# Bringing the second head group's routing chain forward in a list-scheduled attention kernel

## The chip, the cores and the metric

The kernel runs on one core of one Trainium2 chip. The metric is the time on the device in microseconds (us), and lower is better.

## The reference

Attention with 4 batches, 8 heads, 768 rows and 64 columns per head. Each query and key is assigned to the nearest of 16 centroids of its head, and a query sees only keys of its own cluster. The result goes through a gate with a long convolution (projection, convolution over the sequence, product, output projection).

```python
q_assign = np.argmax(np.einsum('bhsd,hcd->bhsc', q_n, c_n), axis=-1)      # q_n, k_n, c_n: normalised
k_assign = np.argmax(np.einsum('bhsd,hcd->bhsc', k_n, c_n), axis=-1)
mask = q_assign[:, :, :, None] == k_assign[:, :, None, :]
scores = np.where(mask, scale * np.matmul(q, k.transpose(0, 1, 3, 2)), -1e9)
attn = softmax(scores)                                                     # cut
x = (attn @ v) in rows of 512
proj = x @ w_proj; x1, x2, x3 = thirds of proj
y = x1 * irfft(rfft(x2) * rfft(filter)) * x3
out = y @ w_out
```

## The kernel before

The eight groups (n = 0 to 7) are four heads each, in two pairs. The kernel does not write its order down. It lists some 1,900 operations, each with an engine (or several to choose from), a guessed duration, a due time and its dependences. A list scheduler simulates the engines and takes, on the engine that is free first, the ready operation with the lowest due time. The order that comes out is what the engines run. The due times are corrected by a table of constants that was found by search, `NUDGE`.

```python
# Plan.op
o.due += NUDGE.get(o.seq, 0.0)
# Plan.place: of the operations that can start now, take the one that is due first
c = min((c for c in cand if c[0] <= t0 + wait + 1e-9), key=lambda c: (
    c[1].due - (bonus if e == "PE" and st.kind == "pv" == c[1].kind else 0.0)
    + (shape if e == "PE" and array(c[1], st.last) != st.last else 0.0)
    + (BUSY if e == "DVE" and len(c[1].eng) > 1 else 0.0) + (c[0] - t0) * 20, c[1].seq))
# Plan.done: when the scheduler believes that a DMA has landed
o.end = st.bw[e] + 0.6 + o.lat
```

The routing chain of a group, for n > 0: similarities of q and k to the centroids on TensorE, transposed on TensorE, the one-hot of the largest on VectorE, a DMA that transposes the one-hot, and eight small DMAs that write its rows ("mask rows") under q and k in the buffers `aug`. A score product over 80 rows (64 of q and k, 16 of the mask) then does the masking. A group's first scores wait for all of this.

```python
# routing(n), cut
b0 = end - 24.00965
op(("PE", 1.33), sim, b0, ...)                    # similarities
op(("PE", .68), simT, b0 + 2.5, ...)              # transposed
...                                               # one-hot on VectorE, due b0 + 3.3 to b0 + 4.2
due = b0 + 7.5
op(("SP", .6), lambda e: T.nc.sync.dma_start_transpose(T.ohT..., T.oh...), due - 2, ..., lat=1.0)
masks(n, range(2), due + 1.3)                     # eight DMAs from ohT to aug, lat=1.0
# the casts that put q and k in aug: whichever of the two engines the scheduler takes
op({"ACT": .83, "DVE": .5}, lambda e, ...: copy(e, T.augs[a][hp][j]..., T.qkT[z]...), due + 8 if n else due + 6, ...)
```

Loads of q, k and v for later groups and the small DMAs of the softmax denominators are issued by SyncE too, in one queue with the transpose and the mask rows.

The softmax here doesn't subtract the row's maximum and nothing guards it: scores larger than these inputs give would overflow.

## Time and profile before

| | before |
|---|---|
| median of 3 runs | 389.62 us (388.48 to 390.36) |
| span of the profiled run | 387.5 us |

The prediction below says how TensorE's idle time is spread over the kernel. It comes from the busy time in windows, two of which follow: the idle time is the stretch less TensorE's busy time, here 40 - 37.80 = 2.20 and 45 - 43.31 = 1.69 us. A line gives the stretch, its length, the busy us of TensorE, of its weight loads, of VectorE, ScalarE and GpSimd (with the number of instructions), the granted clock, the busy share of the DMA engines and their GB/s:

```profile
25.00:65.00 40.00, 37.80 (x299) 18.89 (x297) 34.54 (x42) 31.57 (x62) 2.68 (x5) 1.00 0.73 152
65.00:110.00 45.00, 43.31 (x334) 21.27 (x332) 40.19 (x47) 35.93 (x70) 0.00 (x0) 1.00 0.51 121
```

For comparing orders I use a second measure, the time from the second group's similarity products to the third group's, on TensorE's timeline (start, busy, instruction):

```profile
32.66 1.50 PE L584 MATMUL bank<-qkT,cbd 128*32 128x384 f32 x16
...
73.96 1.50 PE L584 MATMUL bank<-qkT,cbd 128*32 128x384 f32 x16
```

This stage takes 73.96 - 32.66 = 41.30 us, and both of the stops that the prediction starts from lie in it. It is called the second group's stage below.

### The profile page before, as it was taken

To read this page: it belongs to the slowest core of one execution; us is meant where nothing else is said; L and a number is where in the kernel's file an instruction comes from. 1 tells how busy PE (TensorE), PEld (TensorE's weight loads), DVE (VectorE), ACT (ScalarE), POOL (GpSimd) and SP (SyncE) were. 2 spreads that over 40 slices of the span, in tenths; PEclk is the share of its full clock that TensorE was granted. 3 is DMA by queue.
4 is the path that set the end of the run, shared out by engine and by line. 5 is a ranking of instruction groups with operands and counts; after the bars stand their busy time and mean duration, and the time that the engine had idled before them with its cause. 6 is when DMAs were issued, how large, how long until landed. Compare 5 with 4: busy or idle time off the path is not lost.

```text
span 387.5 us, 8477 instructions
## 1 busy us (share of the span) xinstructions
PE 367.5 (95%) x3251; PEld 212.4 (55%) x3256; DVE 353.9 (91%) x509; ACT 269.5 (70%) x514; POOL 46.8 (12%) x92
## 2 busy tenths in 40 slices
PE   2999996999999999999999999999999999999995
PEld 1565452455445555555454555555455566568893
DVE  8898996899799999999998999999999999999782
ACT  5897786788894887788874976778865567632342
POOL 8501000000002010101010100101010100000400
PEclk9999999999999999999999999999999999999999
DMA  9829972750668659866797596845646551110214
GB/s 176 180 65 210 215 170 53 176 142 23 167 125 162 127 83 184 105 147 78 166 162 185 76 246 119 139 90 69 131 64 186 59 162 12 44 43 2 94 72 162
DMA packets 93860, 47.17 MB, mean 122 GB/s; under 512 B 82088, under 2 KB 87676, under 8 KB 93820
## 3 DMA queue, kind: packets, MB, share of 16 engines
q1 hardware_dynamic: 87836, 36.84, 42.1%
q0 software_dynamic: 2704, 8.98, 16.5%
q10 hardware_dynamic: 3280, 0.82, 1.2%
q8 instruction: 25, 0.41, 0.5%
q14 instruction: 15, 0.12, 0.1%
HBM read 31.59 MB, written 7.40 MB: 101 GB/s over the span
## 4 chain that ended last, share of the span: by engine, by line
PE 54%; DVE 24%; DMA 9%; issue 5%; SPq 5%; ACT 3%; DVEq 0%; POOL 0%; POOLq 0%
PE bank L73 19%; PE pair L681 17%; DVE acc L695 8%; PE bank L807 5%; PE bank L71 4%; DMA rb<-dr 3%; PE bank L555 2%; DMA aug<-ohT 2%; PE bank L584 2%; DMA ohT<-oh 2%; SPq L461 2%; DVE tm L831 1%; SPq L746 1%; DVE x L871 1%; SPq L294 1%
## 5 line engine op out<-in xcount | busy, mean ns | idle before, releaser
L681 PE MATMUL pair<-p,vraw 128*64 128x385 f32 x768 | 142.7, 490 | 0.3
L670 ACT ACTIVATE p<-bank 128x512 f32<-128x512 f32 x192 | 113.8, 612 | 36.9 <-PE bank L73 34.4
L695 DVE TENSOR_TENSOR acc<-p,acc 128x1536 f32<-128x1536 f32 x64 | 112.0, 1749 | 3.4 <-ACT p L670 1.1
L681 PEld LDWEIGHTS pair<-p,vraw 128*64 128x64 f32 x768 | 53.0, 136 | 51.0 <-issue 45.8
L73 PE MATMUL bank<-aug,aug 80*64 80x512 bf16 (+3 forms) x590 | 69.0, 327 | 5.2 <-DMA aug<-ohT 3.1
L667 ACT ACTIVATE p<-bank 128x512 f32<-128x512 f32 x96 | 58.8, 612 | 1.7 <-PE bank L73 1.0
L73 PEld LDWEIGHTS <-aug 80*64 80x64 bf16 (+1 forms) x590 | 34.2, 109 | 37.3 <-issue 21.6
L729 POOL DMA_DIRECT2D acc<-acc x30 | 23.8, 795 | 244.1 <-DVE acc L695 81.9
L73 PE MATMUL bank<-xT,wpj 128*64 128x384 bf16 x424 | 41.3, 326 | 0.0
L260 ACT COPY qkT<-bank 128x384 f32<-128x384 f32 x62 | 27.9, 496 | 13.2 <-PE bank L73 8.9
L73 PEld LDWEIGHTS <-wpj 128*64 128x64 bf16 x424 | 27.4, 109 | 13.0 <-issue 7.0
L695 DVE TENSOR_TENSOR acc<-p,p 128x1536 f32<-128x1536 f32 x16 | 28.0, 1750 | 2.1 <-ACT p L670 2.0
L73 PEld LDWEIGHTS <-y 128*64 128x64 bf16 x448 | 24.7, 110 | 8.7 <-issue 3.0
L831 DVE TENSOR_TENSOR tm<-bank,hm 128x512 f32<-128x512 f32 x44 | 27.6, 678 | 0.8 <-ACT p L670 0.4
L260 ACT CAST aug<-qkT 64x768 bf16<-64x768 f32 x29 | 24.0, 830 | 3.0 <-PE bank L73 2.6
L807 PE MATMUL bank<-wpj,xT 128*64 128x512 bf16 x192 | 21.6, 379 | 0.8 <-DVE xT L775 0.8
L73 PE MATMUL bank<-wout,y 128*64 128x512 bf16 x176 | 21.2, 379 | 0.0
L71 PE MATMUL bank<-aug,aug 128*128 128x256 bf16 (+3 forms) x87 | 19.3, 320 | 0.6 <-DVE x L871 0.2
L260 ACT COPY tm<-bank 128x512 f32<-128x512 f32 x14 | 8.0, 589 | 16.1 <-PE bank L807 9.7
L555 PE MATMUL bank<-ident,qkraw 128*128 128x128 f32 x144 | 19.2, 278 | 0.0
L555 PEld LDWEIGHTS bank<-ident,qkraw 128*128 128x128 f32 x144 | 15.6, 140 | 6.3 <-issue 4.2
L262 DVE CAST aug<-qkT 64x768 bf16<-64x768 f32 x31 | 17.6, 572 | 1.5 <-PE bank L73 0.9
(149 smaller groups left out, 434.9 us busy)
## 6 DMA issues: line engine op xcount, KB each, us to landing
vraw<-in_v_dram SPq DMA_DIRECT2D x16, 384.0 KB, 3.5
qkraw<-in_q_dram SPq DMA_DIRECT2D x30, 192.0 KB, 4.8
qkraw<-in_k_dram SPq DMA_DIRECT2D x30, 192.0 KB, 5.2
rb<-dr SPq DMA_DIRECT2D x30, 192.0 KB, 3.6
out_dram<-ob SPq DMA_DIRECT2D x11, 512.0 KB, 3.7
acc<-acc POOLq DMA_DIRECT2D x10, 384.0 KB, 4.9
acc<-acc POOLq DMA_DIRECT2D x10, 192.0 KB, 4.1
y<-in_moe_filter_fft_dram SPq DMA_DIRECT2D x4, 384.0 KB, 7.3
```

Source lines behind the costliest of these rows:

```text
L71: return T.nc.tensor.matmul(out, lhsT, rhs, start=start, stop=stop)
L73: T.nc.tensor.matmul(out[64 * i:64 * i + 64], lhsT[:, 64 * i:64 * i + 64], rhs, start=start, stop=stop)
L260: T.nc.scalar.copy(out, in_)
L262: (T.nc.vector if e == "DVE" else T.nc.gpsimd).tensor_copy(out, in_)
L555: T.nc.tensor.transpose(bank(h.ids[i // 3])[:, ts(i % 3, 128)], raw(s, i), T.ident)
L667: T.nc.scalar.activation(o, ap(h).rearrange("p (a b) -> p a b", a=2), Act.Exp, scale=0.125)
L670: T.nc.scalar.activation(flat(s)[:, lo:lo + 512], ap(h), Act.Exp, scale=0.125)
L681: T.nc.tensor.matmul(o[64 * hp:64 * hp + 64, ch, :385], T.vraw[vs][:, hp, sk * D:(sk + 1) * D], T.p[slots[sk]][:, hp, 384 * ch:384 * ch + ...
L695: T.nc.vector.tensor_tensor(T.acc[os], P_(t[0]), P_(t[1]) if len(t) == 2 else T.acc[os], op=Alu.add)
L729: op(("POOL", .8), lambda e, rows=rows: T.nc.gpsimd.dma_start(flat_()[:rows], flat_()[rows:2 * rows], accum_op=Alu.add), te, r=[], w=[("ac ...
L807: T.nc.tensor.matmul(ap(h)[64 * i:64 * i + 64], T.xT[xs][:, kt, c:c + 64], T.wpj[:, kt, DM:2 * DM], start=kt == 0, stop=kt == ND - 1)
L831: op(("DVE", .68), lambda e, i=i, cs=cs, r=r, h=h: T.nc.vector.tensor_tensor(T.tm[r][:, cs], ap(h), hmrow(i, (0, 2, 2, 3)[2 * r + cs]), op ...
```

## The change

Going by the edit, the intent is to make the second group's one-hot earlier, since its masks come late, and to tell the scheduler that the first transposes and mask rows take longer to land than it believes, so that it issues them sooner. Because every change of the plan moves everything behind it, the due times were then searched for anew.

```diff
-LEAD = 1.97516
+LEAD = 2.99901
-BUSY = 8.32578
+BUSY = 8.09741
+EARLY = 8.73655
-NUDGE = {10:3.7,75:-1.5,90:7.4, ...          (142 entries, cut)
+NUDGE = {6:-0.2,9:0.7,10:3.7,11:-0.3, ...    (271 entries, cut: 136 unchanged, 6 changed, 129 new)
...
-    ... bonus=11.03330, margin=0.02203, shape=1.60501):
+    ... bonus=10.84378, margin=0.02195, shape=1.63806):
...
     # mask rows
-    ... byts=25e3, lat=1.0))
+    ... byts=25e3, lat=2.0 if n < 3 else 1.0))
...
-        b0 = end - 24.00965
+        b0 = end - 24.04235
+        b0 -= EARLY * (n == 1)
...
     # transpose of the one-hot
-    ... byts=196e3, lat=1.0)
+    ... byts=196e3, lat=3.0 if n < 3 else 1.0)
...              (T0, TAU1, w0, w1 moved by under 1 us; w0 of the last batch from -8.47659 to -4.47412)
```

No arithmetic is added or removed. What changes is the order on each engine, and in some cases the engine.

More of the change, by code (lines that the diff above doesn't have):

```diff
@@ L35 @@
 ROWS = 16
-LEAD = 1.97516
+LEAD = 2.99901
 FIRST = 2
-BUSY = 8.32578
+BUSY = 8.09741
 HELD = 4
-NUDGE = {10:3.7,75:-1.5,90:7.4,91:7.4,129:-0.8,140:0.4,156:6.6,187:-5.6,193:0.1,212:-0.2,216:15.5,218:8.0,222:-3.8,243:1.1,253:-4.1,255:-7.1,256:-7.1,257:-3.0,264:4.3,274:2.3,281:0.9,288:9.1,289:11.6,328:-9.2,363:0.5,370:2.2,378:0.5,379:0.7,400:-0.2,406:1.5,409:-4.8,434:0.6,440:-3.7,479:0.8,480:-0.3,481:-1.3,494:-0.6,495:-4.2,508:-1.9,511:-0.2,518:-5.0,524:0.5,526:2.1,539:-2.3,554:10.5,568:1.6,573:0.4,587:-4.9,590:0.2,597:-2.4,617:0.7,620:-1.0,658:0.8,664:0.1,684:2.2,690:-8.8,740:1.0,759:0.5,767:0.4,779:-0.7,782:1.7,788:0.7,790:0.8,826:-0.5,828:-0.3,848:-2.2,872:-1.3,883:-5.3,888:-3.6,897:-0.8,898:-1.1,901:-3.5,915:-3.1,941:0.4,947:-0.4,969:-0.8,996:2.0,997:2.0,1026:2.7,1029:-2.1,1039:2.0,1043:-1.2,1048:1.2,1056:10.8,1062:0.4,1066:0.9,1098:-1.0,1101:0.3,1118:-2.2,1127:1.5,1130:-1.5,1143:-2.6,1194:-0.9,1255:0.7,1257:0.7,1263:0.3,1270:-0.2,1271:-1.1,1276:-3.6,1295:4.9,1317:-2.0,1321:0.4,1351:5.6,1373:-1.5,1441:9.4,1450:3.5,1461:2.0,1478:-1.3,1501:-8.3,1546:0.2,1557:0.1,1563:-0.6,1624:2.8,1630:-1.5,1634:0.3,1640:-4.0,1641:-4.0,1642:-13.7,1643:-4.0,1655:-4.1,1666:0.5,1685:-2.9,1771:-3.3,1776:0.2,1788:-7.8,1797:0.1,1808:-0.1,1809:-0.1,1827:-0.7,1841:-1.3,1844:0.9,1862:-0.4,1863:2.1,1887:2.4,1890:3.2,1898:-7.4,1901:-0.8,1902:-1.5,1903:-0.8,1904:-0.8,1905:-1.8,1906:-1.8}
@@ new lines @@
+EARLY = 8.73655
+NUDGE = {6:-0.2,9:0.7,10:3.7,11:-0.3,71:-0.3,75:-1.5,90:7.4,91:7.4,129:-0.8,140:0.4,152:2.6,155:-6.2,156:6.6,158:-2.3,167:0.6,169:-4.1,187:-5.6,193:0.1,204:0.1,207:-0.7,209:0.8,212:-0.2,216:15.5,218:8.0,222:-3.8,228:-3.1,238:-1.7,239:-1.7,240:-1.7,243:1.1,245:-2.9,253:-4.1,255:-7.1,256:-7.1,257:-3.0,264:4.3,274:2.3,281:0.9,288:9.1,289:11.6,298:0.6,322:-4.8,328:-9.2,329:-0.5,343:0.7,363:0.5,368:-1.5,369:-1.5,370:0.7,371:-1.5,375:0.1,378:0.5,379:0.7,390:-1.8,391:-0.1,400:-0.2,406:2.8,409:-4.8,410:0.5,416:0.2,418:-1.0,433:-11.9,434:0.6,440:-3.7,479:0.8,480:-0.3,481:-0.5,485:1.1,494:-0.6,495:-4.2,504:2.3,508:-1.9,511:-0.2,517:-0.3,518:-5.0,523:-0.4,524:0.5,526:2.1,539:-2.3,547:0.2,554:10.5,558:0.3,565:-0.3,568:1.6,573:0.4,587:-4.9,590:0.2,595:-17.3,597:-2.4,617:0.7,620:-1.0,631:0.3,634:2.8,646:0.7,658:0.8,664:0.1,665:-1.9,684:2.2,690:-8.8,693:2.2,698:0.1,703:-7.8,704:-1.7,705:-1.7,729:0.5,740:1.0,750:-0.6,759:0.5,767:0.4,779:-0.7,782:1.7,784:-0.1,788:0.7,789:-0.3,790:0.8,800:2.5,805:-3.5,810:1.5,822:0.1,824:0.1,826:-0.5,828:-0.3,843:-8.5,848:-1.7,861:0.5,870:2.5,871:2.5,872:-1.3,883:-5.3,888:-3.6,897:-0.8,898:-1.1,901:-3.5,915:-3.1,926:4.0,936:-4.1,937:-3.0,940:2.9,941:0.4,947:-0.4,949:-0.6,969:-0.8,981:1.0,996:2.0,997:2.0,999:-0.3,1026:2.7,1029:-2.1,1031:0.1,1036:3.2,1039:2.0,1043:-1.2,1048:1.2,1050:-0.1,1054:-1.5,1056:10.8,1062:0.4,1066:0.9,1077:-7.7,1083:-3.4,1092:-0.1,1098:-1.0,1101:0.3,1116:-6.9,1118:-4.2,1122:2.8,1123:2.4,1124:2.4,1127:1.5,1130:-1.5,1131:0.3,1132:-2.9,1143:-2.6,1150:4.6,1157:-0.6,1194:-0.9,1236:-2.9,1253:-0.5,1255:0.7,1257:0.7,1263:0.3,1270:-0.2,1271:-1.1,1276:-3.6,1285:2.1,1286:4.6,1295:4.9,1311:-2.5,1317:-2.0,1321:0.4,1322:0.7,1332:-1.9,1337:-0.6,1351:5.6,1357:0.2,1359:0.5,1363:-0.5,1373:-1.5,1374:1.1,1381:0.2,1383:-0.3,1414:-2.7,1419:-0.5,1422:0.3,1425:0.7,1441:9.4,1450:3.5,1461:2.0,1478:-1.3,1479:3.3,1500:1.2,1501:-8.3,1521:0.2,1529:0.8,1546:0.2,1551:-0.2,1552:-1.1,1555:1.4,1557:0.1,1563:-0.6,1591:0.2,1600:-0.4,1619:-4.8,1624:2.8,1630:-1.5,1634:0.3,1640:-4.0,1641:-4.0,1642:-13.7,1643:-4.0,1655:-4.1,1657:0.4,1666:0.5,1672:1.9,1677:-0.3,1680:2.8,1681:2.8,1682:2.8,1685:-2.9,1697:-0.5,1713:-7.0,1741:5.6,1747:13.3,1764:1.1,1771:-3.3,1774:3.4,1776:0.2,1788:-7.8,1797:0.1,1808:-0.1,1809:-0.1,1814:-4.0,1817:-2.0,1823:3.3,1827:-0.7,1841:-1.3,1844:0.9,1859:2.4,1862:2.5,1863:2.1,1865:-0.3,1870:-0.4,1887:2.4,1890:3.2,1898:-7.4,1901:-0.8,1902:-1.5,1903:-0.8,1904:-0.8,1905:-1.8,1906:-1.8}
@@ L110, in op, with place @@
         return o
-    def place(self, free0, banks_for, switch=0.1, wait=0.1, rate=215e3, bonus=11.03330, margin=0.02203, shape=1.60501):
+    def place(self, free0, banks_for, switch=0.1, wait=0.1, rate=215e3, bonus=10.84378, margin=0.02195, shape=1.63806):
         free = dict(free0)
@@ L246, in build @@
     op = P.op
-    T0 = 20.36576
-    TAU1 = 2.98452
+    T0 = 20.38450
+    TAU1 = 2.97769
     TAU2 = 3.43320
@@ L462, in masks @@
                         T.augs[a][hp][j][64 - 64 * hp:80 - 64 * hp], T.ohT[rows]), due + .3 * hp,
-                        r=[("ohT", pr), ("zero", a, j)], w=[("augm", a, hp, j)], byts=25e3, lat=1.0))
+                        r=[("ohT", pr), ("zero", a, j)], w=[("augm", a, hp, j)], byts=25e3, lat=2.0 if n < 3 else 1.0))
         return out
@@ L628, in routing @@
             T.ohT[:].rearrange("p (t n) -> p t n", n=128), T.oh[:].rearrange("p a n c -> p (a n c)")), due - 2,
-           r=both("oh"), w=both("ohT"), byts=196e3, lat=1.0)
+           r=both("oh"), w=both("ohT"), byts=196e3, lat=3.0 if n < 3 else 1.0)
         masks(n, range(2), due + 1.3)
@@ L785, in hyena @@
         last = b == B - 1
-        w0 = A(24 * (b + 1)) + 11.85069
-        w1 = A(24 * (b + 2)) + 50.52404 if b < B - 2 else A(96) + 34.73131
+        w0 = A(24 * (b + 1)) + 11.84958
+        w1 = A(24 * (b + 2)) + 50.56423 if b < B - 2 else A(96) + 35.31752
         if last:
-            w0 = A(96) - 8.47659
+            w0 = A(96) - 4.47412
             w1 = w0 + 10
```

## The prediction

> **What bounds the kernel now.** I read the page first, then the waits of TensorE, then the timelines of TensorE, SyncE's queue and VectorE around the longest waits in mid-kernel. The page says which engine carries the time:
>
> ```profile
> span 387.5 us, 8477 instructions
> PE 367.5 (95%) x3251; PEld 212.4 (55%) x3256; DVE 353.9 (91%) x509; ACT 269.5 (70%) x514; POOL 46.8 (12%) x92
> ```
>
> TensorE is busy 367.5 us of 387.5 and idle 20.0. The matrix work is the same in both kernels, so what a new order can win is that idle time and a few changes of array shape. Read by stretches (busy time per window), the 20.0 us lie so: 8.15 in the first 25 us, 2.2 from 25 to 65, 1.7 from 65 to 110, 3.4 from 110 to 345, 4.6 in the last 42.5. The ends hold 12.7. The order of the instructions of TensorE and ScalarE over some 10 us at the start is unchanged, and the last 35 us of TensorE's order are the same but for the banks' names, so I give the ends no gain. That leaves about 7 us. The view of who waited for whom, for TensorE:
>
> ```profile
> PE bank L565 <- DMA qkraw<-in_q_dram: 5.3, 1, 5.3
> PE bank L73 <- DMA aug<-ohT: 3.1, 3, 1.6
> PE bank L325 <- DVE sd L322: 2.2, 1, 2.2
> PE bank L73 <- DVE den L717: 1.6, 1, 1.6
> PE bank L807 <- DVE xT L775: 0.8, 1, 0.8
> ```
>
> The first and third are the start. The second is a score product waiting for the mask rows that a DMA writes beside q and k. TensorE's timeline, with the idle time in brackets, gives its longest case, at the second group's first score:
>
> ```profile
> 57.77 1.52 PE L681 MATMUL pair<-p,vraw 128*64 128x385 f32 x8
> 60.92 1.50 PE L73 MATMUL bank<-aug,aug 80*64 80x512 bf16 x16 [1.64 <-DMA aug<-ohT]
> ...
> 66.82 0.41 PE L73 MATMUL bank<-aug,aug 128*64 128x512 bf16 x2 [1.61 <-DVE den L717]
> ```
>
> Two stops, 3.25 us together. SyncE's queue shows why the masks come late:
>
> ```profile
> 38.50 7.61 SPq L294 DMA_DIRECT2D qkraw<-in_q_dram  x2
> 46.20 3.56 SPq L294 DMA_DIRECT2D qkraw<-in_k_dram  x2
> 49.81 0.77 SPq L300 DMA_DIRECT2D vraw<-in_v_dram  x1
> 50.68 1.35 SPq L627 DMA_TRANSPOSE ohT<-oh  x1
> 52.13 0.53 SPq L300 DMA_DIRECT2D vraw<-in_v_dram  x1
> 52.76 0.65 SPq L721 DMA_DIRECT2D dd<-den  x1
> 57.12 5.01 SPq L461 DMA_DIRECT2D aug<-ohT  x8
> 62.18 0.61 SPq L723 DMA_DIRECT2D dn<-dd  x1
> ```
>
> VectorE's timeline (same columns) gives the one-hot's end and the second stop:
>
> ```profile
> 41.48 3.43 DVE L417 TENSOR_TENSOR uv<-y,y 128x1536 bf16<-128x1536 f32 x2
> 44.82 0.62 DVE L622 TENSOR_TENSOR oh<-oh,mt 128x384 bf16<-128x384 bf16 x2
> ...
> 64.23 0.23 DVE L742 RECIPROCAL dn<-dn 128x12 f32<-128x12 f32 x1 [3.59 <-DMA dn<-dd]
> 64.48 1.69 DVE L262 CAST aug<-qkT 64x768 bf16<-64x768 f32 x3
> 66.21 0.56 DVE L717 TENSOR_SCALAR den<-bank 128x384 f32<-128x384 f32 x1
> ```
>
> The one-hot is done at 45.4, but its transpose is issued at 50.68, behind loads whose issue alone took 7.61 and 3.56 us: the queue was full, with 210 GB/s moving from 35 to 51. The eight mask rows follow at 57.12, and only behind them the small DMA of the denominators; VectorE waits 3.59 us for that one, does three casts, and only then empties the bank at 66.21. So both stops have one root, the transpose's place in SyncE's queue.
>
> **What the Trainium skill says.** "Perfetto Trace Analysis", section "Identifying the Most-Contended Engine", warns that TensorE's matmul occupancy does not measure distance to the roofline. I use it only to find gaps, and count work by start-to-start times: eight L681 products take 1.30 us in the chain that ended last. "TensorEngine Tiling (Array Packing)", section "Key Properties", says that changing the tiling mode drains TensorE. The trace agrees: the same eight take 1.45 us where a product of another shape went before, so a change costs 0.15 us. "DMA: Bandwidth & Descriptors", section "Issuing engines are not separate DMA queues", says that DMAs from all engines end on the same 16 DMA engines and interleave. That fits here: the weights' loads from GpSimd's queue run in the stretch in which SyncE's issues stall.
>
> **The change part by part.** Durations are of the kernel before; the order of instructions of the changed kernel is known, its times are not.
>
> (1) The second group's transposition of the similarities (L597) moves ahead of one step's scores on TensorE: 3 x 0.215 = 0.65 us earlier, ending near 36.4 instead of 37.05.
>
> (2) On VectorE three casts (1.73 us) leave the place before the one-hot chain, and the pair of filter sums (3.43 us) moves behind it. The chain itself is 1.02 + 1.01 + 0.56 + 0.36 + 0.72 + 0.62 = 4.3 us, so the one-hot is done near 40.7, 4.7 us earlier.
>
> (3) In SyncE's queue the transpose now stands ahead of the two last key loads and one value load. It goes at about 46.2, when the loads before it are issued: 4.5 us earlier. The queue is then the bound, not VectorE.
>
> (4) Those loads now stand between transpose and masks: 46.2 + 1.4 + 3.6 + 0.8 + 0.65 + 0.53 and 0.5 for gaps = 53.6 for the first mask row, against 57.12. If the transpose again takes 6.4 us until the queue goes on, it has landed at 52.6, in time. All eight rows are out by 58.7, and the denominators' DMA follows 3.5 us earlier than before.
>
> (5) So the rows for the first score land near 58.5, and TensorE wants them at about 59.3 plus whatever it has lost by then: the stop of 1.64 goes. The reciprocal is fed by about 60.7, about when VectorE reaches it (60.6 before); the bank is then emptied near 63 instead of 66.8, and of the 1.61 some 0.3 to 0.5 stays. Gain of (1) to (5): 1.64 + 1.2 = 2.8 us.
>
> (6) The price is on ScalarE. It takes over the three casts, so four stand in one row where one stood: 3 x 0.83 = 2.5 us before the exponentials of the second pair's second step. In the kernel before those end near 40, and the copy that frees the output accumulator runs at 40.50. I get 42.9 and 43.7 for them, so the next L681 starts near 43.7, not 41.55. Of these 2.1 us, 0.65 is the denominators' product that moves forward, leaving 1.5 lost. A part comes back, because a stop of 0.44 us at 50 and slack behind it absorb some: I take 0.8 us as the net loss.
>
> (7) Changes of array shape, counted in the order: 82 before, 85 after, + 3 x 0.15 = 0.45 us.
>
> (8) The later groups. The other two mask waits are 0.67 us at 166 (fifth group) and 0.79 at 255 (seventh); 0.78 us of waiting for xT at 209 is the third. In the new order the fifth group's first score comes 1.9 us of TensorE work later and the sixth group's comes 5.2 us earlier, ahead of the 48 products that waited for xT. That should remove 0.67 + 0.78. But in SyncE's queue the broadcast of the denominators (two issues of 0.6) now stands between the masks of the fifth and the seventh group and waits there for another DMA. I charge 1.0 us for that, about the size of one such wait. Net gain 0.45.
>
> The sum: 2.8 - 0.8 - 0.45 + 0.45 = 2.0 us. The re-tuned due times move hundreds of small things that I can't price singly, and they were presumably kept because they helped, so I add 0.6 us as a judgement, not a count: 2.6 us. From the median of 389.62 that gives 387.0.
>
> **The rivals.** (a) ScalarE takes the place of the wait: if (6) costs its full 1.5 to 2.5 us, the gain of the second group is eaten, and the time stays at 388.5 to 390. For it: ScalarE is busy 7.7 of 10 us there and the accumulator has one buffer. Against it: before, it waited 34.4 us in total for TensorE's scores, so it catches up fast. (b) The DMA is the bound: the transpose goes earlier into a queue still full at 210 GB/s, takes longer than 6.4 us, and the stop at 60 stays in part. With half of it left the time is about 388. (c) The whole idle time of mid-kernel goes: with nothing new, up to 7 us, that is 382.6. Against it: every earlier re-order left new short waits, and the retiming of the early chain doesn't act on them. (d) New mask waits in the fifth to seventh group of 2 us each, where the rows stand behind a DMA that waits: 389 to 391.
>
> **Range and chances.** (a) and (b) put the upper end at 389.0, since both can hold in part; a partial (c) puts the lower at 384.6. Faster by over 2% needs less than 381.8, more than all mid-kernel idle time: 0.02. Slower by over 2% needs 8 us of new waits: 0.01. Within 2%: 0.97.
>
> **What would show it.** Right: no wait of the second group's first score on the mask DMA, the transpose issued at 45 to 47 us, the reciprocal not waiting for its DMA, TensorE's idle time from 25 to 110 us down from 3.9 to below 2, ScalarE's four casts in one row near 38 us with L681 behind them some 2 us later than 41.55. Wrong: the transposes taking 9 us or more to land, a new TensorE wait on ScalarE's exponentials or on the accumulator's copy of over 2 us, or mask waits beyond 110 us over 2 us in total. If the span falls by more than 5 us, the cause is not the early chain, and I would look at the windows from 110 us on.

## The result, and the profile after

| | before | after |
|---|---|---|
| median | 389.32 us (388.48 to 390.36, 4 runs) | 387.19 us (387.15 to 387.44, 4 runs) |
| ratio | | 0.9945, 95% interval 0.992 to 0.9971 |
| span of the profiled run | 387.5 us | 385.4 us |
| TensorE idle | 20.0 us | 18.1 us |
| second group's stage | 41.30 us | 39.45 us |

A ratio here is the mean time of one kernel's runs over the mean time of the other's runs of the same rounds, so it is not quite the ratio of the medians beside it. Executions over 1.5% slower than the fastest of the same kernel are left out of the means. The change is 2.1 us by medians: in this test a gain clear of its interval, but within 2%. The second group's stage carries 1.85 of it. The start of the stage carries 0.43, but that moves by more than this between runs of one order (31.73 and 32.23 us in two traces of the changed kernel), so I don't count it. The stages behind add up to a loss of 0.2.

The page of the changed kernel, to be read against the two lines at the head of the prediction:

```profile
span 385.4 us, 8486 instructions
PE 367.3 (95%) x3262; PEld 207.6 (54%) x3267; DVE 352.3 (91%) x504; ACT 273.1 (71%) x519; POOL 46.6 (12%) x92
```

TensorE's work is the same within 0.2 us. ScalarE has 3.6 us more and VectorE 1.6 less: the casts changed engines. Two lines of TensorE's waits after (sum, count, longest):

```profile
PE bank L74 <- ACT p L672: 1.2, 1, 1.2
...
PE bank L74 <- DMA aug<-ohT: 0.4, 1, 0.4
```

The waits for mask rows fell from 3.1 us to 0.4, and the 1.6 on `den` (the softmax denominators, which VectorE copies out of a bank) has left the list. A wait of 1.2 on ScalarE's exponentials is new. TensorE's timeline after shows where it lies:

```profile
39.64 1.04 PE L74 MATMUL bank<-aug,aug 128*64 128x512 bf16 x10
41.92 0.41 PE L74 MATMUL bank<-aug,aug 80*64 80x512 bf16 x2 [1.24 <-ACT p L672]
...
43.59 1.52 PE L683 MATMUL pair<-p,vraw 128*64 128x385 f32 x8
...
58.97 1.52 PE L683 MATMUL pair<-p,vraw 128*64 128x385 f32 x8
60.32 1.04 PE L74 MATMUL bank<-aug,aug 80*64 80x512 bf16 x10
```

The second group's first score now starts at 60.32 right behind the product before it. Both stops of before are gone. The price is at 41.92, where a score wants a bank that ScalarE has not emptied. ScalarE's timeline before and then after shows why:

```profile
38.50 0.83 ACT L260 CAST aug<-qkT 64x768 bf16<-64x768 f32 x1
...
40.50 0.80 ACT L699 COPY osb<-pair 128x770 f32<-128x770 f32 x1 [0.55 <-PE pair L681]
```

```profile
37.89 3.35 ACT L261 CAST aug<-qkT 64x768 bf16<-64x768 f32 x4
...
42.72 0.82 ACT L701 COPY osb<-pair 128x770 f32<-128x770 f32 x1
```

Four casts stand in a row where one stood, and the copy that frees the output accumulator runs 2.2 us later. SyncE's queue after:

```profile
37.78 7.67 SPq L295 DMA_DIRECT2D qkraw<-in_q_dram  x2
45.55 3.68 SPq L629 DMA_TRANSPOSE ohT<-oh  x1
49.33 1.26 SPq L295 DMA_DIRECT2D qkraw<-in_k_dram  x2
...
52.59 5.75 SPq L462 DMA_DIRECT2D aug<-ohT  x8
58.38 0.61 SPq L725 DMA_DIRECT2D dn<-dd  x1
```

The transpose goes out at 45.55 instead of 50.68, and mask rows and denominators follow 4.5 and 3.8 us earlier. VectorE after:

```profile
39.41 0.63 DVE L624 TENSOR_TENSOR oh<-oh,mt 128x384 bf16<-128x384 bf16 x2
...
60.53 0.23 DVE L744 RECIPROCAL dn<-dn 128x12 f32<-128x12 f32 x1
...
62.52 0.56 DVE L719 TENSOR_SCALAR den<-bank 128x384 f32<-128x384 f32 x1
```

The reciprocal no longer waits (3.59 before), and the bank is emptied at 62.52 instead of 66.21. One point stands out. The one-hot is finished at 40.04, but the transpose still waits in the queue until 45.55, behind q loads. (That the queue is "full" there, as the prediction says, is a reading of these issue times; no view shows how full it is. The weights' loads from GpSimd, which the prediction names beside it, were moved by no run, so what holds the issues up is not tested.) The windows after:

```profile
25.00:65.00 40.00, 37.78 (x297) 18.95 (x298) 35.81 (x45) 34.04 (x64) 2.61 (x5) 1.00 0.79 163
65.00:110.00 45.00, 44.54 (x343) 23.71 (x341) 38.75 (x44) 37.24 (x71) 0.90 (x1) 1.00 0.50 119
```

Idle time from 25 to 110 us is 2.22 + 0.46 = 2.68 us, against 3.89. From 110 to 345 it is 235 - 232.05 = 2.95 against 3.38.

### The profile page after: what moved, and what is told of

The parts are those of the page before. It is cut to its first block, busy times and chain, and to the rows that moved or that the text cites. A ratio compares the mean times of both kernels' runs of the same rounds, so it can differ in the third digit from the quotient of the medians.

```text
span 385.4 us, 8486 instructions
## 1 busy us (share of the span) xinstructions
PE 367.3 (95%) x3262; PEld 207.6 (54%) x3267; DVE 352.3 (91%) x504; ACT 273.1 (71%) x519; POOL 46.6 (12%) x92
## 3 DMA queue, kind: packets, MB, share of 16 engines
q1 hardware_dynamic: 87836, 36.84, 42.5%
## 4 chain that ended last, share of the span: by engine, by line
PE 65%; DVE 19%; ACT 6%; issue 4%; DMA 3%; SPq 1%; POOL 0%; DVEq 0%; ACTq 0%; POOLq 0%
PE bank L74 24%; PE pair L683 21%; DVE acc L697 6%; PE bank L809 5%; PE bank L72 4%; PE bank L556 3%; ACT p L672 2%; PE bank L586 2%; DMA dr<-dn 2%; DMA aug<-ohT 2%; ACT aug L261 2%; DVE tm L833 2%; PE bank L599 1%; PE bank L451 1%; PE bank L566 1%
## 5 line engine op out<-in xcount | busy, mean ns | idle before, releaser
L683 PE MATMUL pair<-p,vraw 128*64 128x385 f32 x768 | 142.5, 490 | 0.2
L683 PEld LDWEIGHTS pair<-p,vraw 128*64 128x64 f32 x768 | 54.2, 136 | 47.8 <-issue 41.1
L74 PE MATMUL bank<-aug,aug 128*64 128x512 bf16 (+3 forms) x580 | 68.4, 328 | 2.1 <-ACT p L672 1.2
L669 ACT ACTIVATE p<-bank 128x512 f32<-128x512 f32 x96 | 58.6, 611 | 6.2 <-PE bank L74 5.6
L74 PEld LDWEIGHTS <-aug 128*64 128x64 bf16 (+1 forms) x580 | 34.4, 109 | 34.5 <-issue 22.4
L74 PE MATMUL bank<-xT,wpj 128*64 128x384 bf16 x440 | 42.7, 326 | 0.0
L74 PEld LDWEIGHTS <-wpj 128*64 128x64 bf16 x440 | 25.5, 109 | 15.9 <-issue 6.4
L74 PEld LDWEIGHTS <-y 128*64 128x64 bf16 x464 | 22.9, 110 | 12.6 <-issue 4.4
L261 ACT CAST aug<-qkT 64x768 bf16<-64x768 f32 x33 | 27.3, 829 | 2.5 <-PE bank L74 1.7
L72 PE MATMUL bank<-aug,aug 80*128 80x256 bf16 (+3 forms) x92 | 20.0, 321 | 0.2
L701 ACT COPY osb<-pair 128x770 f32<-128x770 f32 x16 | 12.9, 809 | 6.9 <-PE pair L683 6.8
```

The costliest lines, as they stand in the source:

```text
L72: return T.nc.tensor.matmul(out, lhsT, rhs, start=start, stop=stop)
L74: T.nc.tensor.matmul(out[64 * i:64 * i + 64], lhsT[:, 64 * i:64 * i + 64], rhs, start=start, stop=stop)
L261: T.nc.scalar.copy(out, in_)
L669: T.nc.scalar.activation(o, ap(h).rearrange("p (a b) -> p a b", a=2), Act.Exp, scale=0.125)
L683: T.nc.tensor.matmul(o[64 * hp:64 * hp + 64, ch, :385], T.vraw[vs][:, hp, sk * D:(sk + 1) * D], T.p[slots[sk]][:, hp, 384 * ch:384 * ch + ...
L701: op(("ACT", .83), lambda e: T.nc.scalar.copy(T.osb[o3], two(ob)[:, :, :385]), te, r=[ob], w=[("osb", o3)], free=[ob])
```

## The experiments

The theory to test: the whole gain comes from one thing, the transpose's place in SyncE's queue, and the three casts on ScalarE are a price paid for the earlier one-hot. The rivals: the earlier one-hot is what counts; the searched due times of the later groups are what counts; or it is only noise.

The edits marked "reorder" leave the plan alone and move single operations in its finished order, with a check that everything that an operation depends on still stands ahead of it. `behind(order, ops, x)` puts `ops` just behind `x`.

All times are medians of 6 runs, slow ones among them, in us. (Without the slow ones b_both has 390.1 and its before 388.0.) "Stage" is the second group's stage in the profiled run.

| run | median (lowest to highest) | ratio to before, 95% | stage |
|---|---|---|---|
| before_again | 389.0 (388.05 to 389.74) | 1.0025 [0.9984, 1.0065] | 40.58 |
| after_again | 387.21 (386.63 to 388.39) | 0.9984 [0.9963, 1.0005] | 39.65 |
| b_swap | 386.45 (385.19 to 387.53) | 0.9962 [0.994, 0.9984] | 38.14 |
| b_swap_again | 386.94 (386.18 to 388.06) | 0.9958 [0.9923, 0.9993] | 39.82 |
| a_unswap | 389.71 (387.49 to 390.81) | 1.0042 [1.0015, 1.0069] | 40.75 |
| a_casts_dve | 389.03 (388.54 to 390.43) | 1.0036 [1.0013, 1.006] | 41.94 |
| a_casts_dve2 | 388.17 (387.28 to 389.08) | 1.0002 [0.9962, 1.0043] | 40.48 |
| b_swap_casts | 388.98 (386.8 to 392.54) | 1.0041 [0.9976, 1.0105] | 39.13 |
| b_both | 390.86 (388.96 to 394.81) | 1.0062 [1.0012, 1.0111] | 39.65 |
| b_early | 392.23 (390.17 to 394.53) | 1.009 [1.0048, 1.0133] | 39.02 |
| b_lat | 394.74 (392.53 to 397.14) | 1.0155 [1.011, 1.02] | 40.63 |
| b_swap2 | 388.44 (386.43 to 390.55) | 0.9982 [0.9931, 1.0034] | 39.98 |

Three calls, each with its own runs of before: after_again, b_swap, a_unswap and a_casts_dve (before: 388.0, from 386.63 to 389.31); before_again, a_casts_dve2, b_swap_casts and b_both (388.45, from 385.61 to 392.3, a noisy one); b_early, b_lat, b_swap2 and b_swap_again (389.32, from 386.08 to 390.49).

**Both kernels again, unaltered.**

> Control: the kernel before, unaltered, for a second trace of it and the noise of the method. Expected ratio 1.000 within 0.0025; the transpose issued at 50 to 51 us, stops of 1.2 to 2 us on the mask rows at the second group and on the denominators' bank.

> Control: the changed kernel unaltered, on the same chip as the three that follow. Expected 387.2 us, ratio to the kernel before 0.9945, the second group's transpose issued near 45.5 us, no stop of TensorE on the mask rows at the second group, the four casts in one row on ScalarE near 38 us.

The stage is 40.58 and 39.65 in these traces. With the first pair, 41.30 and 39.45, the gain of the stage is 0.9 to 1.85 us, 1.4 between the means. By the median the changed kernel was only 0.8 us ahead, and the interval includes 1. So the whole gain was 2.1 us in one test and 0.8 in the other, where no gain at all is within the interval; its size stays open. Before again has both stops, in another split (0.74 on the masks, which is less than expected, and 1.80 on `den`); after again has neither, and the same 1.24 on ScalarE.

**b_swap: the kernel before, with only the transpose moved in SyncE's queue.**

```diff
 # reorder: the second group's transpose (tr), one place in one engine's order
+tr = pick(order, ("ohT", 1))
+order = behind(order, pick(order, ("qk", 2, 1, 1), ("v", 1, 0)), tr[0])   # two key loads, one value load
```

> The kernel before with one instruction moved: the second group's one-hot transpose stands ahead of the last two key loads and one value load in SyncE's queue; nothing else differs on any engine. Theory 1 (both stops of 1.64 and 1.61 us have one root, the transpose's place in that queue): transpose issued near 46.2, first mask row near 53.6, both stops gone but for 0 to 0.4 us, no price on ScalarE, so 2.8 to 3.2 us faster, ratio near 0.9925, faster than the changed kernel by about 1 us. Rival A (the queue is full and the transpose only lands later): it takes 9 us or more to land and the gain is under 1 us. Rival B (the gain of the changed kernel is spread over the re-tuned due times): gain under 0.7 us.

SyncE's queue, VectorE's one-hot and TensorE's only wait on `den` in it:

```profile
44.69 4.11 SPq L667 DMA_TRANSPOSE ohT<-oh  x1
48.91 1.26 SPq L327 DMA_DIRECT2D qkraw<-in_k_dram  x2
...
52.21 5.93 SPq L498 DMA_DIRECT2D aug<-ohT  x8
```

```profile
44.04 0.62 DVE L661 TENSOR_TENSOR oh<-oh,mt 128x384 bf16<-128x384 bf16 x2
```

```profile
62.88 0.41 PE L73 MATMUL bank<-aug,aug 128*64 128x512 bf16 x2 [0.17 <-DVE den L758]
```

In this trace, of the fastest of the six runs, one moved operation removes both stops but for 0.17 us, and the stage falls from 41.30 to 38.14. The one-hot is nearly as late as before (done at 44.66), and the transpose goes at once. No cast changed engines and no due time was touched. The median, 386.45, is the lowest of its call. But the time missed what was expected: the ratio of 0.9962 is 1.5 us and not 2.8 to 3.2. The next run shows why.

**b_swap_again: the same kernel, on another chip.**

> Repeat of b_swap beside the others on the same chip, to see whether one moved instruction beats the changed kernel again. Expected stretch from the second to the third group's similarities 38.1 us (kernel before 40.6 to 41.3, changed kernel 39.5 to 39.7), ratio to the kernel before 0.992 to 0.997.

The ratio repeats, 0.9958 after 0.9962, but the expected stage of 38.1 us doesn't: it is 39.82. The profiled run was this time the slowest of the six (388.06), and it shows the limit of the repair:

```profile
59.50 1.50 PE L73 MATMUL bank<-aug,aug 80*64 80x512 bf16 x16 [0.86 <-DMA aug<-ohT]
...
64.71 0.41 PE L73 MATMUL bank<-aug,aug 128*64 128x512 bf16 x2 [0.92 <-DVE den L761]
```

The eight mask rows took 6.90 us to issue instead of 5.93, and half of the stops is back. The trace of b_swap2 below, whose second group has the same order, agrees: 7.42 us for the rows, stops of 1.02 and 0.92, a stage of 39.98. So two traces of three keep 1.78 and 1.94 us of the two stops, where the traces of before have 3.25 and 2.54, and only the best is free of them. The mean stage of the three is 39.31, against 40.94 for the two of before and 39.55 for the two of after. Why the rows are slower in some runs stays open. The changed kernel has more room here. It wants the rows at 60.32, not at 58.6 (59.50 - 0.86), because its casts on ScalarE have delayed it. A part of that price thus covers a wait that would otherwise be there.

**a_unswap: the changed kernel, with only the transpose put back behind those loads.**

```diff
 # reorder
+order = behind(order, tr, pick(order, ("v", 1, 0))[0])
```

> The changed kernel with the transpose put back behind the key loads and the value load, nothing else altered. Theory 1: transpose near 50, first mask row near 56.5, a stop of 0.5 to 1.5 us on the mask rows at the second group's first score and another of 0.5 to 1.5 us on the denominators' bank come back, so 1.5 to 2.5 us slower than the changed kernel, ratio to the kernel before 0.998 to 1.001. Rival B: under 0.7 us slower than the changed kernel.

The time is 2.5 us over after_again by medians, and slower than before. SyncE's queue, and TensorE's first score of the second group and its wait on `den`:

```profile
45.23 4.29 SPq L328 DMA_DIRECT2D qkraw<-in_k_dram  x2
...
50.34 1.33 SPq L669 DMA_TRANSPOSE ohT<-oh  x1
```

```profile
60.58 1.04 PE L74 MATMUL bank<-aug,aug 80*64 80x512 bf16 x10
...
64.72 0.55 PE L593 MATMUL bank<-ident,qkraw 128*128 128x128 f32 x3 [1.07 <-DVE den L760]
```

The one-hot is done at 40.29 on VectorE's timeline, and the transpose goes out ten microseconds later. The stop on `den` is back with 1.07 us. The stop on the masks, which was expected too, is not: the first score starts without a wait (the trace's mask waits, 0.42 and 0.65, are at 208 and 255 us). The stage is 1.10 us longer than after_again's and 1.30 longer than after's. It is 40.75, about what before has, so the earlier one-hot alone is worth nothing that shows here; its price on ScalarE, the same 1.24, remains. Of the 1.9 us between the two profiled runs (387.4 and 385.5), 1.10 is in the stage, 0.75 ahead of it, where nothing was moved, and 0.05 behind it. The 2.5 of the medians thus overstates what the move did.

**a_casts_dve and a_casts_dve2: the changed kernel, with three of the four casts back on VectorE.** Two places were tried, behind the one-hot chain and behind the last addition of the first pair's sums.

```diff
 # reorder
+casts = pick(order, ("cast", 1, 1, 0, 0), ("cast", 1, 1, 0, 1), ("cast", 1, 1, 1, 0))
+for o in casts:
+    o.on = "DVE"
+order = behind(order, casts, pick(order, ("oh2", 1, 0))[0])      # a_casts_dve
+order = behind(order, casts, pick(order, ("acc", 0, 0, 5))[0])   # a_casts_dve2
```

> The changed kernel with three of the four casts given back to VectorE, behind the one-hot chain; ScalarE keeps one. Tests step 6, the price on ScalarE. If the four casts in a row cost TensorE 0.8 to 1.5 us: the wait of a score product on the exponential (1.24 us at 41.9) goes and the time is 386.0 to 386.5, ratio near 0.992. If VectorE becomes the bound there (the filter sums come 1.7 us later and the spectrum products wait for them): no gain or up to 0.5 us slower than the changed kernel.

> The changed kernel with three casts on VectorE, now behind the last addition of the first pair's sum and ahead of the filter sums. In a_casts_dve they stood ahead of that addition, and the denominators' product waited 2.59 us for it. If step 6's price on ScalarE is real and VectorE has room here: the 1.24 us wait of a score product on the exponential goes, no wait over 0.5 us takes its place between 36 and 52 us, and the time is 0.7 to 1.2 us below the changed kernel (386.0 to 386.5 where that is 387.2). If VectorE has no room: the spectrum products or the filter products wait 1 us or more, and the time is that of the changed kernel or above.

In both the price was to come back if VectorE had room, and it didn't: it moved. TensorE's waits in the first and then in the second:

```profile
42.86 0.85 PE L754 MATMUL bank<-acc,ones 128*32 128x384 f32 x8 [2.59 <-DVE acc L740]
```

```profile
51.08 1.49 PE L490 MATMUL bank<-uv,fw 128*64 128x512 bf16 x12 [1.63 <-DVE hm L477]
```

In the first the casts delay the sums that the denominators' product needs; in the second the product on the filter waits 1.63 us for VectorE. The second also shows that the 1.24 us of waiting on an exponential were not the casts alone: with three of them gone from ScalarE, 0.96 of such a wait stays, ahead of the denominators' product (41.79). Neither place has 1.7 us of room, and by the stage ScalarE was the best of the three tried. The first run lost more than its wait: behind the stop of 2.59 us the granted clock fell to 0.82 and 0.50 in two stretches of 2.5 us (42.5 to 47.5), which is 2.5 x (0.18 + 0.50) = 1.7 us of full-clock time. Without it its stage would have been about 40.2 and not 41.94.

**b_swap_casts: b_swap, with the three casts moved to ScalarE.** This adds only the price.

```diff
 # reorder, on top of b_swap
+for o in casts:
+    o.on = "ACT"
+order = before_(order, casts, pick(order, ("cast", 1, 1, 1, 1))[0])   # just ahead of the fourth
```

> The kernel before with the transpose moved as in b_swap and, besides, the three casts moved from VectorE to ScalarE in one row with the fourth. Against b_swap it shows the price of step 6 alone. Step 6 says the L681 after the casts starts about 2 us later and TensorE loses 0.8 to 1.5 us net, so 0.8 to 1.5 us slower than b_swap (387.2 to 388 where that is 386.45). Rival: ScalarE's slack absorbs it, within 0.4 us of b_swap.

```profile
42.17 1.52 PE L726 MATMUL pair<-p,vraw 128*64 128x385 f32 x8 [1.67 <-ACT osb L745]
```

The predicted stop on the accumulator's copy is there, with 1.67 us. The stage is 39.13, 0.99 over b_swap's, but 0.69 under b_swap_again's and 0.85 under b_swap2's. So the stop is shown; a net price is not. It is 1.0 against the one trace without late masks, and none against the other two, where the rows come later than a delayed TensorE would want them. The times can't decide it: three runs at 386.8 to 387.4, at a granted clock of 1.0, and three at 390.6 to 392.5, at 0.988 to 0.996 (see b_swap2).

**b_both, b_early, b_lat: the kernel before with parts of the change, and the old due times.**

```diff
+        b0 -= 8.73655 * (n == 1)                             # b_early and b_both
-    ... byts=25e3, lat=1.0))
+    ... byts=25e3, lat=2.0 if n < 3 else 1.0))               # b_lat and b_both, mask rows
-    ... byts=196e3, lat=1.0)
+    ... byts=196e3, lat=3.0 if n < 3 else 1.0)               # b_lat and b_both, transpose
```

> The kernel before with the second group's chain due 8.74 us earlier and the longer landing times told to the scheduler, all other due times old (no re-tuned list, no shifted stage constants). The order shows the transpose ahead of the last key loads, as in the changed kernel. If the transpose's place is what counts and the re-tuned times add little: ratio 0.994 to 0.998, no mask stop at the second group. If the re-tuned times are needed to keep the later groups in step: new waits beyond 75 us of 1 us or more and a ratio of 1.000 or above.

> The kernel before with the second group's chain due 8.74 us earlier and nothing else. Its order has the transpose ahead of the last key loads, but the denominators' DMA behind the mask rows. Theory 1: the mask stop at the second group goes; the stop on the denominators' bank stays or grows to 2 us or more, because its DMA now goes out after the masks; stretch between the second and the third group's similarities 39.5 to 41 us. Later groups out of step as in b_both: stretch from third to seventh above 200.

> The kernel before with only the landing times told to the scheduler changed (3 and 2 us for the first three groups), due times old. Its order has the transpose ahead of the last key loads and the three casts still on VectorE ahead of the one-hot chain, so no price on ScalarE. Theory 1: both stops go, stretch between the second and the third group's similarities 38 to 39 us, near b_swap's; if so the scheduler's landing time alone does the work and the 8.74 us are not needed.

All three bring the transpose forward in the queue (43.50, 45.34 and 46.40 us), and in none does the second group's first score wait for its masks. The stage is 39.65 with both, 39.02 with the earlier due time alone, 40.63 with the longer landing times alone. Two details missed: b_early was to keep its stop on `den` and has none, and b_lat was to have 38 to 39. Yet all three are slower than before. What follows the second group's stage, to the end of the profiled run, takes 387.5 - 73.96 = 313.5 us before and 385.4 - 71.68 = 313.7 after. In b_both it is 316.9, in b_early 321.7, in b_lat 320.3. One wait of b_early shows the kind:

```profile
167.78 0.41 PE L73 MATMUL bank<-aug,aug 80*64 80x512 bf16 x2 [3.38 <-DMA aug<-ohT]
```

Behind it the clock dips as in a_casts_dve, for another 1.7 us. (b_lat has such a dip too, in the second group's stage: 1.7 of its 40.63, which would else be 38.9.) A list scheduler that is told something new about the second group also lays out the groups behind it anew, and the old corrections no longer fit. The searched due times and scheduler constants, taken together, are thus needed for the plan to hold, and they add nothing of their own that the traces show.

**b_swap2: b_swap, and the same idea for the fifth and seventh group**, whose masks were 0.67 and 0.79 us late.

```diff
 # reorder, on top of b_swap: a load goes behind the first two mask rows
+order = behind(order, pick(order, ("qk", 5, 1, 1)), first[-1])   # fifth group: two key loads
+order = behind(order, pick(order, ("v", 6, 1)), first[-1])       # seventh group: one value load
```

> b_swap with two more moves in SyncE's queue alone: in the fifth group two key loads go behind the first two mask rows, in the seventh one value load does. Theory: the mask waits of 0.35 and 0.99 us that b_swap has there shrink by 0.3 and 0.5 us or go; stretch from the third group's similarities to the seventh's 0.5 to 0.9 us shorter than b_swap's 199.26, time 0.3 to 0.8 us under b_swap's. If the rows' landing is set by something else (the transpose still under way): no change.

Inconclusive, and no better. The six runs fall in two clusters, 386.4 to 386.7 and 390.2 to 390.6, and the profile is of the second. The late masks of these two groups are gone there (the second group's were told above), and two waits on VectorE stand in their place, one of 1.13 us at 174.82 and this one:

```profile
180.59 1.44 PE L71 MATMUL bank<-inv,y 128*128 128x192 bf16 x8 [2.59 <-DVE qkT L301]
```

Ahead of both, VectorE had stood 3.76 us for the DMA that broadcasts the denominators (0.61 in the kernel before). And the stop has a second price. The windows around it, with the granted clock as the third column from the right:

```profile
177.50:180.00 2.50, 0.49 (x4) 0.19 (x2) 2.43 (x4) 1.29 (x3) 0.76 (x1) 1.00 0.38 39
180.00:182.50 2.50, 1.91 (x11) 1.25 (x12) 2.50 (x4) 0.01 (x1) 0.00 (x0) 0.52 0.16 28
182.50:185.00 2.50, 2.50 (x14) 1.08 (x16) 2.04 (x3) 1.26 (x3) 0.00 (x0) 0.80 0.71 163
```

The clock falls to about half for some 3.4 us: 2.5 x (0.48 + 0.20) = 1.7 us of full-clock time. A stop of 2.59 and a dip of 1.7 are 4.3 together, and the clusters lie 3.8 apart. The runs of the slow cluster have a mean clock of 0.989 to 0.996 and those of the fast one 0.998 to 1.0, and b_swap_casts splits at the same place (one dip of 1.7 in 388 us is 0.004). So the slow cluster is most likely the runs in which some stop grew long enough for a dip; no trace of the fast cluster of b_swap2 or of the slow one of b_swap_casts exists to compare. Why the broadcast is late in some runs stays open.

## Why the prediction was right

The time, 387.0 predicted and 387.19 measured, was right for mostly the reason given. By its own steps:

- **(1) to (3), the earlier chain and the transpose.** Predicted one-hot at 40.7 and transpose at 46.2; measured 40.04 and 45.55. "The queue is then the bound, not VectorE" held: the transpose went 5.5 us after the one-hot. What the prediction did not conclude from its own sentence is that the earlier one-hot then buys nothing. b_swap (late one-hot, new place) and a_unswap (early one-hot, old place) show it. So do the queues: counted from the stage's start, the transpose goes out at 11.7 us in b_both, at 12.8 in b_swap, at 13.3 in after and at 13.9 in b_swap_again, and the first mask row at 20.5, 20.3, 20.4 and 20.9 (b_lat's, with 14.3, at 22.2). An earlier transpose is only longer at its issue (5.37 us in b_both).
- **(4), the rows.** Predicted first row at 53.6 and denominators at 58.7, measured 52.59 and 58.38. The parts were wrong and their sum right: the transpose was to take 1.4 us to issue and the key loads 3.6, and they took 3.68 and 1.26, 4.94 together against 5.0. So the stall seems to belong to the queue, and to meet whichever DMA is next in it.
- **(5), both stops.** Predicted gain 2.8, leaving 0.3 to 0.5 of the second. In the changed kernel none is left, 3.25 us less waiting. In b_swap's order, where it stands alone, the stage gained 3.16 in the best trace. In b_swap_again it gained 1.48 against the first trace of before and 0.76 against the second; between the means of three traces and two it is 1.6. So 2.8 was near the upper end.
- **(6), the price on ScalarE.** Predicted 0.8 net; 0.99 against the best trace of b_swap, and nothing against the two others, so the size is not shown. It showed as 1.24 us of waiting on an exponential, ahead of the accumulator that the prediction named, and L683 started at 43.59 as predicted (43.7). It fell short of rival (a).
- **(7), the changes of array shape**, 0.45: too small to be told apart. TensorE's busy time differs by 0.2 us the other way.
- **(5) to (7) together**: 2.8 - 0.8 - 0.45 = 1.55 predicted, 1.85 in the first pair of traces and 0.93 in the second.
- **(8) and the judgement**, 0.45 + 0.6 = 1.05: this is the term that was off. From the end of the stage to the end of the run the kernels take 313.5 and 314.6 us before, 313.7 and 314.1 after, which is nothing that stands out of the spread. The fifth group's mask wait and the one for `xT` did go, and the charge of 1.0 for a broadcast in the way did not fall due. But the seventh group's mask wait stayed with 0.45, and 0.76 at 164 and 0.73 at 342 came anew:

```profile
164.43 0.85 PE L74 MATMUL bank<-inv,y 128*64 128x192 bf16 x16 [0.76 <-DVE x L873]
...
253.04 0.41 PE L74 MATMUL bank<-aug,aug 80*64 80x512 bf16 x2 [0.45 <-DMA aug<-ohT]
```

- **The sum.** 2.6 predicted, 2.1 in the first test and 0.8 in the second. The nearness to 387.0 is in part luck: a start of the stage that came 0.43 us earlier by chance stood in for a part of the 1.05 that did not come.
- **The signs.** All held but one: the idle time from 25 to 110 us was to fall below 2 and is 2.68, because of the 1.24 on ScalarE and three waits of 0.37 to 0.48 that no step had (at 50.13, 52.41 and 92.48 us, where before had one of 0.44 that the prediction hoped to absorb).
- **The rivals.** (b), half of the mask stop left by a slow DMA, did not happen in the changed kernel, but is what b_swap_again and b_swap2 show in another order. (c) and (d) did not happen.

The kernel before with one instruction moved, b_swap, did at least as well as the whole change: 386.45 against 387.21. The intervals of the two ratios overlap and the mean stages are 0.2 us apart, so "better" is not shown, but it needs neither the new due times nor the casts' move.

## What to carry to other kernels

When a wait is traced to a DMA, look at where that DMA stands in its queue before making its input earlier: here the input lay ready for five microseconds, and one move in the queue did the work of 135 new or changed due times. Where a scheduler lays out the program, try the suspected order by hand on the finished plan, because a change of the scheduler's inputs moves everything behind it and mixes the effects. And before an operation goes to the engine that looks idle, or back, find the place in the timeline where it fits, since busy shares don't show it. A stop of 1.5 to 3.4 us in mid-kernel cost 1.7 us more than its length through the clock in four of the traces, while stops of 1.6 to 1.8 in others cost nothing more.

## What the Trainium skill lacked or had wrong

- "DMA: Bandwidth & Descriptors", section "Issuing engines are not separate DMA queues", says that the sequencer's time to start a DMA "is usually small relative to the DMA itself". Here two loads of 192 KB held SyncE for 7.67 us at their issue, while the median landing time of such loads in the same run was 4.1 us. The page has no time for issue on SyncE that is held up behind earlier DMAs, and does not say that the delay passes to the DMA that comes next: the key loads took 3.56 us behind the q loads and 1.26 behind the transpose, the transpose 1.35 and 3.68.
- "DMA: Bandwidth & Descriptors", section "Latency and other measured facts", gives 261 GB/s for a DMA transpose, measured on one kernel with a non-contiguous middle dimension. From that, the 196,608 bytes of this one-hot (128x768 in 2 bytes) would take an estimated 0.75 us. The seven transposes here took a median of 3.7 us to land in the kernel before and 4.8 in the changed one, so in a busy queue the rate says little. The page has no landing time for a transpose.
- "TensorE: Matmul & The Clock Gate", section "What's actually happening", says that the array falls to half clock after at least one idle window of about 3.4 us. The half clock and the length agree: four dips here cost 1.7 us each, which is 3.4 us at half. But the stops ahead of them were shorter than the window: 2.59 us in a_casts_dve and b_swap2, 3.38 in b_early, and in b_lat 1.51 with 0.32 ahead of it. Stops of 1.64 and 1.61 in the profile of before had no dip, nor had the wait of 5.33 us at the very start. So, by these runs, a stop shorter than the page's figure is not safe, and they don't fix another limit.
